# Attention scores: blocks of three and of one share a PSUM bank, value products of those two together, and a new table of leans

## The chip, the cores and the metric

The kernel runs on one core of one Trainium2 chip. The metric is the time in microseconds (us) of one execution on the device. Before the change it is 1697.37 us, the median of three runs (1695.88, 1697.37 and 1698.11).

## What is computed

Four layers act in turn on x, 2048 rows of 512 numbers, each added to its input: attention with a memory, a Fourier mixing, and the two once more. In the reference, cut to what matters:

```
x = x + A(layernorm(x)); x = x + B(layernorm(x))      # twice
A: q, k, v of 32 heads, 16 wide; 4 segments of 512 rows, in turn:
     p     = softmax(q k^T * scale + causal mask)       # inside the segment
     a_mem = phi(q) M / (phi(q) z + 1e-6)
     o     = g * a_mem + (1 - g) * (p v)
     M, z  = M + phi(k)^T v, z + sum phi(k)
   return o wo
B: y = dft_seq_re (x dft_hid_re^T) - dft_seq_im (x dft_hid_im^T)
```

Inside a segment the mask keeps a key block only for the query blocks at and behind it. With blocks of 128 rows there are four key blocks and four query blocks, and a head has ten blocks of scores that count, of the sixteen.

## The kernel before

A segment's 32 heads are worked in four groups of eight; a group is four pairs (p) of two heads (a = 0 or 1). There are 2 layers x 4 segments x 4 groups = 32 groups. Each group's q and k stand in `qst` and `kst` so that head a of a pair lies on partitions from 64a on, and the products of the two heads run side by side in the TensorE's upper and lower rows (called row-tiled below). The scores are computed twice. `s_x` computes them with the queries on the partitions, and the VectorE takes each row's maximum (`t_max`, whose tiles are `junk` and `mx`). One transpose by the TensorE (`identf,mx`) turns the maxima, which then become two more rows of `qst`. `s_st` computes the scores once more with the keys on the partitions, the maximum subtracted. For each PSUM bank the ScalarE takes the exponential into a tile `pt` (in profiles `w`), and the GpSimd sets the masked triangle of each diagonal block to zero (`t_sel`, an affine select).

`s_av` multiplies v by these tiles: 32 output partitions for each pair, four pairs in the four column strips of the array (column-tiled below; `w,vt` in profiles). All four key blocks t of a group add up in one bank `av` for each a. Everything else of the TensorE (projections, the hidden and the sequence DFT, the output projection, each with 128 rows and 128 columns) uses the whole array, in f16 pairs. Matmuls that fill gaps (`onesb`) keep the TensorE's clock up while little work is ready.

A step of `s_x` and of `s_st` fills two banks, one for each a, and both passes walk over t. A product of block t is n = 128 (t+1) columns wide in `s_x`, and n = 512 - 128 t in `s_st`, and a bank of 512 columns takes as many pairs as fit:

```
for t in range(TT):
    n = 512 - 128 * t
    w = 512 // n
    for p0 in range(0, NP, w):
        yield need("T", qs, ks, tag=(kt, kt, "pt", "pt"), mode="h")
```

So the width of 512 takes four steps, 384 takes four, 256 takes two and 128 takes one: 11 steps a group and pass, of which the four of width 384 leave a quarter of their banks empty. `s_av` takes a step for each t and a, that is 8 a group.

The order on every engine is set when the program is built. Streams (`s_...`) and tasks (`t_...`) are Python generators that say which engine, tiles and PSUM banks they need next; a planner with costs and due times (`Plan`) keeps the time at which each is free, and the loop at the end of `body` lets the candidate go that could begin first. The table `LEAN` is subtracted there: a number of planned ns for a stream and an engine's letter (V, A, G, T, Y: VectorE, ScalarE, GpSimd, TensorE, SyncE's DMA queue), positive to be taken earlier, negative later. The planner also charges a change between whole-array, row-tiled and column-tiled work (`mode`). Every instruction is recorded through one helper line (L272 before, L273 after), so rows of the profile are told apart by their tiles.

Of the kernel before, what the change touches and what calls it, by code (L numbers as in the profile page):

```python
# [13 lines left out]
OP = mybir.AluOpType  # L14
# [15 lines left out]
BF16 = mybir.dt.bfloat16  # L30
NEG = -1e30
TICK = 10240 / 3
LEAN = dict(s_stT=150.0, s_memV=40.0, s_wV=80.0, s_rY=150.0, t_mergeA=40.0, s_xA=150.0, t_abA=40.0, t_mergeY=-150.0, s_mV=40.0, t_cV=-40.0, s_cA=-80.0, s_oY=40.0, t_cY=80.0, t_lnG=80.0, t_splitV=-40.0, t_phiA=150.0, s_kV=-300.0, t_mergeV=150.0, s_cT=80.0, s_avT=80.0, s_wA=-150.0, t_resV=-150.0, t_selG=40.0, s_lnY=-150.0, t_rowsY=300.0, t_ktY=-80.0)
APART = dict(pj=(1, 4), av=(1, 2), dft=(0, 2), sx=(2, 4), st=(2, 4), ss=(0, 4))
SHARED = dict(pj=(1, 4), av=(0, 2), dft=(1, 2), sx=(0, 2), st=(0, 2), ss=(2, 6))
HOLD, SWITCH = 700.0, 95.0
# [7 lines left out]
WARM, IDLE, SPARE = 4200, 500.0, 300.0  # L44
DEEP = 1500.0
AHEAD = 2
NR = 2


# [229 lines left out]
def body(ctx: ExitStack, tc: tile.TileContext, x, wq, wk, wv, wo, beta, wd, cs, out):  # L279
# [23 lines left out]
    def ps(kind, dt=F32, shape=(128, 512)):  # L303
        return pl.take(kind, shape, dt)
# [62 lines left out]
    def spawn(g):  # L367
        tasks.append([next(g, None), g, g.__name__])
# [44 lines left out]
    def share(o, src, s):  # L413
# [3 lines left out]
        yield need("VG", o, src)  # L417
        tt(o[:, 1], src, o[:, 0], OP.subtract)

    def flat(t):  # L420
        return t.rearrange("p a b -> p (a b)")

# [228 lines left out]
    def t_merge(e, o, gi, g, n, key):  # L651
        yield gate("GM")
        yield need("V", e, o, gt, tag="md")
        x = sb("md", F32, (128, 2, 512))
        V.transpose(x[:, 0], e)
        yield need("V", x)
        V.transpose(x[:, 1], o)
        pl.close(e, o)
        rc = rg("rc", 4, F32, (128, 2, 16))
        xa = x[:, 0]  # L660

        def view(off, *dims):
            return bass.AP(xa.tensor, xa.offset + off, [list(xa.ap[0])] + [list(d) for d in dims])

        yield need("V", x)
        d = view(16, (496, 2), (32, 16))
        if not gi:
            V.tensor_scalar(rc, d, 1e-6, None, op0=OP.add)
            d = rc
        V.reciprocal(rc, d)  # L670
        yield need("G", rc)
        G.tensor_tensor(rc, rc, gt[:, gi, g, :].unsqueeze(2).to_broadcast([128, 2, 16]), op=OP.mult)
        yield need("VG", rc, x)
        for a in range(2):
            c = slice(16 * a, 16 * a + 16)
            tt(n.rearrange("p (b r) -> p b r", r=32)[:, :, c], view(528 * a, (32, 16), (1, 16)),
               rc[:, a].unsqueeze(2).to_broadcast([128, 16, 16]), OP.mult)
        pl.close(x)
        done.add(key)
# [201 lines left out]
        apart[0] = False  # L881
        kinds.update(SHARED)

    def t_max(sp, mx, a, p0, w, t, left):
        n = 128 * (t + 1)
        for p in range(p0, p0 + w):
            o = (p - p0) * n
            yield need("V", sp)
            junk = rg("junk", 2, BF16)
            V.tensor_tensor_reduce(junk[:, :n], sp[:, o:o + n], cmask[:, 512 - n:], 1.0, -3e38,  # L890
                                   OP.add, OP.max, mx[:, a, p, t:t + 1])
        pl.close(sp)
        left[0] -= 1

    def s_x():
        for i in range(NGRP):
            yield gate(("dq", i), ("dk", i), "CM")
            qs, ks = qst[i % NR], kst[i % NR]
            mx = rg("mx", 2, F32, (128, 2, NP, TT))
            left = [0]  # L900
            kx = scores("x")
            for t in range(TT):
                n = 128 * (t + 1)
                w = 512 // n
                for p0 in range(0, NP, w):
                    yield need("T", qs, ks, tag=(kx, kx), mode="h")
                    sp = [ps(kx), ps(kx)]
                    for p in range(p0, p0 + w):
                        o = (p - p0) * n
                        for a in range(2):  # L910
                            T.matmul(sp[a][:, o:o + n], qs[64 * a:64 * a + 48, p, 128 * t:128 * t + 128],
                                     ks[64 * a:64 * a + 48, p, 0:n], start=True, stop=True)
                    left[0] += 2
                    for a in range(2):
                        spawn(t_max(sp[a], mx, a, p0, w, t, left))
# [12 lines left out]
            for a in range(2):  # L928
                for j in range(2):
                    r = 64 * a + 48 + j  # L930
                    Y.dma_start(qs[r:r + 1].rearrange("o p (t n) -> o (p t) n", t=TT),
                                mhl[16 * a:16 * a + 16, j, :], est=(609, 341, 172))
            done.add(("X", i))

    def t_sel(sp, pt, w, n, f, keys):
        yield need("A", sp)
        A.activation(pt[:, :w * n], sp[:, :w * n], AF.Exp, scale=f)
        pl.close(sp)
        yield need("G", pt)
        v3 = pt[:, :w * n].rearrange("k (w n) -> k w n", w=w)[:, :, 0:128]  # L940
        G.affine_select(v3, v3, pattern=[[0, w], [1, 128]], compare_op=OP.is_ge, fill=0.0,
                        base=0, channel_multiplier=-1)
        for k in keys:
            done.add(k)

    def s_st():
        for i in range(NGRP):
            yield gate(("X", i), "KR")
            qs, ks = qst[i % NR], kst[i % NR]
            kt = scores("t")  # L950
            for t in range(TT):
                n = 512 - 128 * t
                w = 512 // n
                for p0 in range(0, NP, w):
                    yield need("T", qs, ks, tag=(kt, kt, "pt", "pt"), mode="h")
                    sp = [ps(kt), ps(kt)]
                    for p in range(p0, p0 + w):
                        o = (p - p0) * n
                        for a in range(2):
                            T.matmul(sp[a][:, o:o + n], ks[64 * a:64 * a + 50, p, 128 * t:128 * t + 128],  # L960
                                     qs[64 * a:64 * a + 50, p, 128 * t:], start=True, stop=True)
                    for a in range(2):
                        pt = sb("pt")
                        spawn(t_sel(sp[a], pt, w, n, f_s[i % NG], [("pt", i, a, t, p) for p in range(p0, p0 + w)]))
                        for p in range(p0, p0 + w):
                            pts[i, a, t, p] = (pt, pt[:, (p - p0) * n:(p - p0 + 1) * n])
            done.add(("ST", i))

    def s_av():
        for i in range(NGRP):  # L970
            q, g = divmod(i, NG)
            v = vt[i % NR]
            for t in range(TT):
                for a in range(2):
                    yield gate(("v", i), *[("pt", i, a, t, p) for p in range(NP)])
                    tiles = [pts[i, a, t, p] for p in range(NP)]
                    yield need("T", v, *[x[0] for x in tiles], tag="av" if t == 0 else (), mode="v")
                    if t == 0:
                        avs[i, a] = ps("av")
                    av = avs[i, a]  # L980
                    for p in range(NP):
                        T.matmul(av[32 * p:32 * p + 32, 128 * t:],
                                 v[:, t, p].rearrange("k e d -> k (e d)")[:, 16 * a:16 * a + 32], tiles[p][1],
                                 start=(t == 0), stop=(t == TT - 1), skip_group_check=True)
                    for x in {x[0].tensor.name: x[0] for x in tiles}.values():
                        pl.close(x)
            done.add(("E", i))

# [339 lines left out]
```

## Time and profile before

| what | value |
|---|---|
| median of three runs | 1697.37 us |
| profiled execution, its own time | 1699.92 us |
| its span, from first to last instruction | 1698.2 us |
| VectorE, ScalarE, GpSimd busy | 1036.8, 872.3, 810.3 us |
| matmul records of the TensorE | 11145 |
| transposes of maxima on the TensorE: start of the first and the fifth | 48.26 and 185.19 us |

A row of the groups' view names engine, operation, tiles (out<-in), shapes, the count, then busy us and mean ns of one, and the engine's idle time ahead of them. The trace lists each f32 matmul twice (1024 products of v in the program stand as 2048). Matmuls overlap in the pipeline, so the distance between two starts, not the duration shown, is what a matmul takes of the TensorE's time.

### The profile page before, as it was taken

How to read it: one execution, taken by the hardware profiler on the slowest of the kernel's cores; microseconds unless marked ns; L12 is line 12 of the kernel's file. 1: busy time of each engine (PE TensorE's matmuls, PEld its weight loads, DVE VectorE, ACT ScalarE, POOL GpSimd, SP SyncE). 2: the span in 40 equal slices, each digit the busy share in tenths (PEclk: the TensorE clock that was granted, in tenths of full speed). 3: DMA queues.
4: the chain of work that ended last, by engine and by line, in shares of the span. 5: the costliest groups of instructions: out<-in, count | busy, mean ns of one | idle time of the engine just before them, and what ended most of it. 6: DMA issues, size and time to landing. Idle time of an engine off the chain costs nothing.

```text
span 1698.2 us, 32247 instructions
## 1 busy us (share of the span) xinstructions
PE 1662.3 (98%) x11145; PEld 734.7 (43%) x11145; DVE 1036.8 (61%) x3262; ACT 872.3 (51%) x1480; POOL 810.3 (48%) x1445
## 2 busy tenths in 40 slices
PE   8889999999999999999999999999999999999999
PEld 4344344444444344444544444443444444444444
DVE  8784865778677786635768558546575765433221
ACT  5487577755656666535376754655455325312000
POOL 4376556575565556634255644635454415322000
PEclk9789999999999999999999999999999999999999
DMA  7546545655357432525746663543435322131423
GB/s 182 147 116 178 128 132 159 172 142 152 94 148 208 126 119 84 189 56 196 193 148 187 182 179 90 132 116 98 140 91 149 105 85 76 57 125 38 143 70 123
DMA packets 208629, 222.92 MB, mean 131 GB/s; under 512 B 104520, under 2 KB 127048, under 8 KB 208464
## 3 DMA queue, kind: packets, MB, share of 16 engines
q1 hardware_dynamic: 208464, 220.85, 45.8%
q8 instruction: 88, 1.44, 0.4%
q14 instruction: 77, 0.63, 0.1%
HBM read 137.40 MB, written 61.87 MB: 117 GB/s over the span
## 4 chain that ended last, share of the span: by engine, by line
PE 77%; DVE 9%; ACT 5%; issue 4%; DMA 3%; POOL 2%; SPq 1%; ACTq 0%; DVEq 0%; POOLq 0%
PE b L272 77%; ACT w L272 4%; DVE junk L272 4%; SPq L272 1%; DVE w L272 1%; POOL w L272 1%; DMA w<-w 1%; DMA w<-x 1%; DVE m L272 1%; DVE mx L272 1%; DVE y L272 1%; DVE bst L272 0%; DVE cam L272 0%; DMA w<-in_cs_dram 0%; DVE pmax L272 0%
## 5 line engine op out<-in xcount | busy, mean ns | idle before, releaser
L272 PEld LDWEIGHTS <-w 128*128 128x128 f16 x5056 | 467.8, 98 | 612.8 <-issue 101.1
L272 PE MATMUL b<-w,w 128*128 128x512 f16 x3072 | 708.5, 380 | 1.7 <-DVE mx L272 0.8
L272 ACT ACTIVATE w<-b,fac 128x512 f32<-128x512 f32 (+1 forms) x728 | 419.2, 655 | 176.3 <-PE b L272 175.8
L272 DVE CUSTOM_DVE_ANT_0 junk<-b,cmask 128x128 bf16<-128x128 f32 (+3 forms) x1024 | 436.3, 483 | 71.6 <-PE b L272 71.1
L272 POOL TENSOR_TENSOR w<-w,w 128x512 f16<-128x512 f32 (+1 forms) x294 | 347.5, 1187 | 247.1 <-ACT w L272 223.6
L272 POOL TENSOR_SCALAR_AFFINE_SELECT w<-w 128x128 f32<-128x128 f32 (+2 forms) x704 | 237.0, 350 | 202.7 <-ACT w L272 194.1
L272 DVE SCALAR_TENSOR_TENSOR y<-b,fyu,y 128x512 f32<-128x512 f32 x200 | 148.9, 745 | 235.6 <-PE b L272 235.2
L272 ACT ACTIVATE w<-w,csc 128x512 f16<-128x512 f32 (+1 forms) x256 | 180.1, 720 | 41.5 <-DVE csc L272 32.8
L272 PE MATMUL b<-g,w 128*128 128x512 f16 x768 | 183.1, 383 | 3.2 <-DMA g<-w 0.8
L272 PE MATMUL b<-wd,w 128*128 128x512 f16 x768 | 176.8, 379 | 0.1
L272 PE MATMUL b<-w,vt 128*32 128x512 f32 (+3 forms) x2048 | 172.4, 449 | 1.9 <-POOL w L272 1.1
L272 ACT ACTIVATE w<-b 128x512 f16<-128x512 f32 x128 | 75.9, 596 | 189.4 <-PE b L272 179.3
L272 DVE SCALAR_TENSOR_TENSOR w<-b,w 128x512 f16<-128x512 f32 x128 | 87.6, 687 | 120.3 <-ACT w L272 118.7
L272 ACT ACTIVATE w<-w 128x512 f16<-128x512 f32 (+1 forms) x137 | 86.5, 632 | 90.1 <-DVE w L272 87.9
L272 PE MATMUL b<-kst,qst 48*128 48x128 f16 (+3 forms) x1024 | 117.5, 304 | 6.3 <-DVE mx L272 3.2
L272 PE MATMUL b<-qst,kst 50*128 50x512 f16 (+3 forms) x1024 | 115.8, 302 | 5.5 <-DVE mx L272 2.2
L272 PE MATMUL b<-w,g 128*128 128x128 f16 x1536 | 96.3, 221 | 0.0
L272 PEld LDWEIGHTS <-g 128*128 128x128 f16 x1536 | 89.6, 99 | 12.7 <-issue 7.8
L272 DVE STREAM_TRANSPOSE m<-b 128x512 f32<-128x512 f32 x112 | 75.6, 698 | 31.1 <-PE b L272 30.7
L272 PEld LDWEIGHTS b<-w,vt 128*32 128x32 f32 x2048 | 54.8, 110 | 87.7 <-issue 48.2
L272 PE MATMUL b<-wo,w 128*128 128x512 f16 x384 | 89.1, 379 | 0.0
L272 PEld LDWEIGHTS <-kst 50*128 50x128 f16 x1024 | 37.3, 94 | 111.7 <-issue 105.2
(105 smaller groups left out, 1019.3 us busy)
## 6 DMA issues: line engine op xcount, KB each, us to landing
w<-in_cs_dram SPq DMA_DIRECT2D x128, 256.0 KB, 3.5
cc<-w SPq DMA_DIRECT2D x128, 256.0 KB, 3.2
w<-cc SPq DMA_DIRECT2D x128, 256.0 KB, 3.1
w<-w SPq DMA_DIRECT2D x96, 256.0 KB, 3.5
d<-w SPq DMA_DIRECT2D x128, 128.0 KB, 2.5
w<-in_x_dram SPq DMA_DIRECT2D x32, 256.0 KB, 3.6
qst<-d SPq DMA_DIRECT2D x64, 128.0 KB, 2.7
kst<-d SPq DMA_DIRECT2D x64, 128.0 KB, 3.3
```

What stands on the lines that cost most here:

```text
L272: r = f(*args, **kw)
```

## The change

Both passes now have steps of three kinds, built by `steps`: `a` is the block of width 512, one pair a bank; `b` is width 256, two pairs a bank; `c` puts width 384 at column 0 and width 128 of the same pair at column 384. That is 4 + 2 + 4 = 10 steps a group and pass. `s_x` takes them in the order a, b, c, so the widest come first where the narrowest did; `s_st` in the order a, c, b. `s_av` takes a step for each kind and a: 6 a group, and the step of kind c does the products of key blocks 1 and 3 together, 8 matmuls after each other. `t_sel` takes one exponential over the whole bank and one affine select over all the diagonal blocks in it, with a view that steps from column 0 to 384. `view` is only moved out of `t_merge`. In `LEAN`, `t_resV` goes from -150 to -300 and `t_selG` from 40 to -150, `s_lnY` (-150) goes, and `s_mA` (-80), `s_xY` (-40) and `t_yA` (-150) come.

```diff
-LEAN = dict(... t_resV=-150.0, t_selG=40.0, s_lnY=-150.0, t_rowsY=300.0, t_ktY=-80.0)
+LEAN = dict(... t_resV=-300.0, t_selG=-150.0, t_rowsY=300.0, t_ktY=-80.0, s_mA=-80.0, s_xY=-40.0, t_yA=-150.0)
+XORDER, SORDER = "abc", "acb"
...
+    def steps(span):
+        one, two, four = (sorted(range(TT), key=lambda t: span(t)[1])[i] for i in (0, 1, 3))
+        three = 6 - one - two - four
+        return dict(
+            a=[[(four, p, 0)] for p in range(NP)],
+            b=[[(two, p, 0), (two, p + 1, 256)] for p in range(0, NP, 2)],
+            c=[[(three, p, 0), (one, p, 384)] for p in range(NP)])
...
-    def t_sel(sp, pt, w, n, f, keys):
+    def t_sel(sp, pt, items, f, keys):
         yield need("A", sp)
-        A.activation(pt[:, :w * n], sp[:, :w * n], AF.Exp, scale=f)
+        n = items[-1][2] + 512 - 128 * items[-1][0]
+        A.activation(pt[:, :n], sp[:, :n], AF.Exp, scale=f)
         pl.close(sp)
         yield need("G", pt)
-        v3 = pt[:, :w * n].rearrange("k (w n) -> k w n", w=w)[:, :, 0:128]
+        v3 = view(pt, 0, (max(items[-1][2], 1), len(items)), (1, 128))
...
     def s_av():
...
-            for t in range(TT):
+            for k in SORDER:
                 for a in range(2):
-                    yield gate(("v", i), *[("pt", i, a, t, p) for p in range(NP)])
+                    ts = sorted({t for x in SSTEP[k] for t, p, o in x})
+                    yield gate(("v", i), *[("pt", i, a, t, p) for t in ts for p in range(NP)])
```

Counted over the whole order of both programs (a run is a stretch of TensorE matmuls of one tiling):

| | before | after |
|---|---|---|
| steps of each score pass x banks | 352 x 2 | 320 x 2 |
| exponentials of scores on the ScalarE | 704 | 640 |
| affine selects on the GpSimd | 704 | 640 |
| steps of value products | 256 | 192 |
| matmuls that fill gaps (`onesb`, 512 columns) | 83 | 85 |
| row-tiled runs on the TensorE | 378 | 359 |
| column-tiled runs | 119 | 104 |
| whole-array runs | 363 | 354 |

The order of the TensorE, in the middle of the kernel, between the 19th and the 20th transpose of maxima: value products of key block 1 (32x384) of one group, for a = 0 and then a = 1, with `b` the bank `av` and `w` the tiles of exponentials. Before:

```order
L272 MATMUL b_12927<-w_12961,vt_108 32x384
L272 MATMUL b_12927<-w_12967,vt_108 32x384
L272 MATMUL b_12927<-w_13005,vt_108 32x384
L272 MATMUL b_12927<-w_13012,vt_108 32x384
L272 MATMUL b_12935<-w_12962,vt_108 32x384
L272 MATMUL b_12935<-w_12968,vt_108 32x384
L272 MATMUL b_12935<-w_13006,vt_108 32x384
L272 MATMUL b_12935<-w_13013,vt_108 32x384
```

The same place after the change, a = 0 and the first row of a = 1:

```order
L273 MATMUL b_12779<-w_12814,vt_108 32x384
L273 MATMUL b_12779<-w_12830,vt_108 32x384
L273 MATMUL b_12779<-w_12869,vt_108 32x384
L273 MATMUL b_12779<-w_12879,vt_108 32x384
L273 MATMUL b_12779<-w_12814,vt_108 32x128
L273 MATMUL b_12779<-w_12830,vt_108 32x128
L273 MATMUL b_12779<-w_12869,vt_108 32x128
L273 MATMUL b_12779<-w_12879,vt_108 32x128
L273 MATMUL b_12796<-w_12815,vt_108 32x384
```

The four products of key block 3 (32x128), which stood in a later run with those of block 2, now follow those of block 1, and read the same four tiles.

The order of the TensorE near the kernel's start, in the first group's pass for the maxima: a row-tiled step (`kst,qst`; the bank's two heads alternate) and the gap-filling matmuls behind it. Before:

```order
L272 LDWEIGHTS qst_106
L272 MATMUL b_819<-kst_104,qst_106 128x384
L272 LDWEIGHTS qst_106
L272 MATMUL b_820<-kst_104,qst_106 128x384
L272 LDWEIGHTS onesb
L272 MATMUL b_827<-onesb 128x512
L272 LDWEIGHTS onesb
L272 MATMUL b_827<-onesb 128x512
L272 LDWEIGHTS onesb
L272 MATMUL b_827<-onesb 128x512
```

After, a step of kind c there:

```order
L273 LDWEIGHTS qst_106
L273 MATMUL b_811<-kst_104,qst_106 128x384
L273 LDWEIGHTS qst_106
L273 MATMUL b_812<-kst_104,qst_106 128x384
L273 LDWEIGHTS qst_106
L273 MATMUL b_811<-kst_104,qst_106 128x128
L273 LDWEIGHTS qst_106
L273 MATMUL b_812<-kst_104,qst_106 128x128
L273 LDWEIGHTS onesb
L273 MATMUL b_827<-onesb 128x512
```

The products of width 128 (`128x128`), which opened the pass with eight in one step, now stand behind each pair of width 384, in the same two banks.

The order of the GpSimd in the middle of the kernel, one group's selects and the f16 splits (TENSOR_TENSOR) around them. Before, from the last two selects of a group's blocks of width 384 on:

```order
L272 AFFINE_SELECT w_11966<-w_11966 128x128
L272 AFFINE_SELECT w_11967<-w_11967 128x128
L272 TENSOR_TENSOR w_11997<-w_11708,w_11997 128x512
L272 TENSOR_TENSOR w_12013<-w_11733,w_12013 128x512
L272 AFFINE_SELECT w_12022<-w_12022 128x2x128
L272 AFFINE_SELECT w_12023<-w_12023 128x2x128
L272 AFFINE_SELECT w_12037<-w_12037 128x2x128
L272 AFFINE_SELECT w_12038<-w_12038 128x2x128
L272 AFFINE_SELECT w_12055<-w_12055 128x512
L272 AFFINE_SELECT w_12056<-w_12056 128x512
```

After, from the last two selects of the banks of kind c on:

```order
L273 AFFINE_SELECT w_11807<-w_11807 128x2x128
L273 AFFINE_SELECT w_11808<-w_11808 128x2x128
L273 TENSOR_TENSOR w_11842<-w_11253,w_11842 128x512
L273 TENSOR_TENSOR w_11872<-w_11521,w_11872 128x512
L273 AFFINE_SELECT w_11884<-w_11884 128x2x128
L273 AFFINE_SELECT w_11885<-w_11885 128x2x128
L273 AFFINE_SELECT w_11898<-w_11898 128x2x128
L273 AFFINE_SELECT w_11899<-w_11899 128x2x128
L273 TENSOR_TENSOR w_11936<-w_11556,w_11936 128x512
```

The two selects over four blocks (`128x512`) are gone, since the blocks of width 128 now lie beside those of width 384, and those selects cover two blocks each; what stands between them is the same kind of work.

More of the change, by code (lines that the diff above doesn't have):

```diff
@@ L418, in share, with view @@
         tt(o[:, 1], src, o[:, 0], OP.subtract)
+    def view(t, off, *dims):
+        return bass.AP(t.tensor, t.offset + off, [list(t.ap[0])] + [list(d) for d in dims])
     def flat(t):
@@ L659, in t_merge @@
         rc = rg("rc", 4, F32, (128, 2, 16))
-        xa = x[:, 0]
-        def view(off, *dims):
-            return bass.AP(xa.tensor, xa.offset + off, [list(xa.ap[0])] + [list(d) for d in dims])
         yield need("V", x)
-        d = view(16, (496, 2), (32, 16))
+        d = view(x, 16, (496, 2), (32, 16))
         if not gi:
@@ L675, in t_merge @@
             c = slice(16 * a, 16 * a + 16)
-            tt(n.rearrange("p (b r) -> p b r", r=32)[:, :, c], view(528 * a, (32, 16), (1, 16)),
+            tt(n.rearrange("p (b r) -> p b r", r=32)[:, :, c], view(x, 528 * a, (32, 16), (1, 16)),
                rc[:, a].unsqueeze(2).to_broadcast([128, 16, 16]), OP.mult)
@@ L882, in together, with t_max @@
         kinds.update(SHARED)
[L884 to L887, printed above, removed]
+    def steps(span):
[5 more added lines that the diff above has]
+            c=[[(three, p, 0), (one, p, 384)] for p in range(NP)])
+    XSTEP = steps(lambda t: (0, 128 * (t + 1)))
+    SSTEP = steps(lambda t: (128 * t, 512 - 128 * t))
+    def t_max(sp, mx, a, items, left):
+        for t, p, o in items:
+            n = 128 * (t + 1)
             yield need("V", sp)
@@ L901, in s_x @@
             kx = scores("x")
-            for t in range(TT):
[L903 to L913, printed above, removed]
-                    for a in range(2):
-                        spawn(t_max(sp[a], mx, a, p0, w, t, left))
+            for items in [x for k in XORDER for x in XSTEP[k]]:
+                yield need("T", qs, ks, tag=(kx, kx), mode="h")
+                sp = [ps(kx), ps(kx)]
+                for t, p, o in items:
+                    n = 128 * (t + 1)
+                    for a in range(2):
+                        T.matmul(sp[a][:, o:o + n], qs[64 * a:64 * a + 48, p, 128 * t:128 * t + 128],
+                                 ks[64 * a:64 * a + 48, p, 0:n], start=True, stop=True)
+                left[0] += 2
+                for a in range(2):
+                    spawn(t_max(sp[a], mx, a, items, left))
             yield lambda: left[0] == 0
@@ L950, in s_st @@
             kt = scores("t")
[L951 to L961, printed above, removed]
-                    for a in range(2):
[L963 to L966, printed above, removed]
+            for items in [x for k in SORDER for x in SSTEP[k]]:
+                yield need("T", qs, ks, tag=(kt, kt, "pt", "pt"), mode="h")
+                sp = [ps(kt), ps(kt)]
+                for t, p, o in items:
+                    n = 512 - 128 * t
+                    for a in range(2):
+                        T.matmul(sp[a][:, o:o + n], ks[64 * a:64 * a + 50, p, 128 * t:128 * t + 128],
+                                 qs[64 * a:64 * a + 50, p, 128 * t:], start=True, stop=True)
+                for a in range(2):
+                    pt = sb("pt")
+                    spawn(t_sel(sp[a], pt, items, f_s[i % NG], [("pt", i, a, t, p) for t, p, o in items]))
+                    for t, p, o in items:
+                        pts[i, a, t, p] = (pt, pt[:, o:o + 512 - 128 * t])
             done.add(("ST", i))
@@ L972, in s_av @@
             v = vt[i % NR]
-            for t in range(TT):
+            for k in SORDER:
                 for a in range(2):
-                    yield gate(("v", i), *[("pt", i, a, t, p) for p in range(NP)])
-                    tiles = [pts[i, a, t, p] for p in range(NP)]
-                    yield need("T", v, *[x[0] for x in tiles], tag="av" if t == 0 else (), mode="v")
-                    if t == 0:
+                    ts = sorted({t for x in SSTEP[k] for t, p, o in x})
+                    yield gate(("v", i), *[("pt", i, a, t, p) for t in ts for p in range(NP)])
+                    tiles = {(t, p): pts[i, a, t, p] for t in ts for p in range(NP)}
+                    yield need("T", v, *[x[0] for x in tiles.values()], tag="av" if k == SORDER[0] else (), mode="v")
+                    if k == SORDER[0]:
                         avs[i, a] = ps("av")
                     av = avs[i, a]
[L981 to L985, printed above, removed]
+                    for t in ts:
+                        for p in range(NP):
+                            T.matmul(av[32 * p:32 * p + 32, 128 * t:], v[:, t, p].rearrange("k e d -> k (e d)")[:, 16 * a:16 * a + 32], tiles[t, p][1],
+                                     start=(k == SORDER[0]), stop=(k == SORDER[-1] and t == ts[-1]),
+                                     skip_group_check=True)
+                    for x in {x[0].tensor.name: x[0] for x in tiles.values()}.values():
                         pl.close(x)
```

4 lines of the change are left out of this document (2 added, 2 removed).

## The prediction

> **What bounds the kernel now.** First the page: busy time of each engine, and the chain that ended last.
>
> ```profile
> PE 1662.3 (98%) x11145; PEld 734.7 (43%) x11145; DVE 1036.8 (61%) x3262; ACT 872.3 (51%) x1480; POOL 810.3 (48%) x1445
> PE 77%; DVE 9%; ACT 5%; issue 4%; DMA 3%; POOL 2%; SPq 1%; ACTq 0%; DVEq 0%; POOLq 0%
> ```
>
> The matmuls cover 98% of the span and carry 77% of the chain. A share over the whole span hides stages, so next the table by stretch: from the first scores (34 us) to the fifth transpose of maxima (185 us), from there to 1361 us, and the rest.
>
> ```profile
> 34.00:185.00 151.00, 137.43 (x986) 57.65 (x983) 109.97 (x421) 100.74 (x175) 87.68 (x160) 0.89 0.56 149
> 185.00:1361.00 1176.00, 1163.71 (x8152) 514.90 (x8152) 778.66 (x2488) 686.85 (x1165) 643.41 (x1132) 1.00 0.50 140
> 1361.00:1698.20 337.20, 333.22 (x1803) 146.73 (x1803) 117.98 (x266) 64.17 (x111) 62.22 (x124) 1.00 0.28 88
> ```
>
> The columns are us, then busy us and count of PE, PEld, DVE, ACT and POOL, the granted clock, and the DMA. In the long middle PE stands still for 12.3 us of 1176, at full clock. In the start it stands still for 13.6 of 151 us, and the clock is 0.89. The view of waits says for whom PE waited, over the span:
>
> ```profile
> PE b L272 <- DVE mx L272: 10.6, 19, 1.6
> PE b L272 <- ACT w L272: 5.1, 13, 0.9
> PE b L272 <- POOL w L272: 3.0, 9, 0.8
> ```
>
> These are score banks that the VectorE or the ScalarE had not emptied (15.7 us) and value products whose tile GpSimd had not masked (3.0 us). So over the middle the kernel takes as long as PE's queue takes, and what counts is how long the same products occupy PE. The timeline of PE shows it, row after row (start, us, tiles):
>
> ```profile
> 400.32 1.07 PE L272 MATMUL b<-w,vt 128*32 128x256 f32 x16
> 401.33 1.47 PE L272 MATMUL b<-w,w 128*128 128x512 f16 x6
> 402.73 0.55 PE L272 MATMUL b<-kst,qst 48*128 48x384 f16 x4
> 403.21 2.12 PE L272 MATMUL b<-w,w 128*128 128x512 f16 x9
> 405.26 0.64 PE L272 MATMUL b<-w,vt 128*32 128x128 f32 x16
> 405.84 0.60 PE L272 MATMUL b<-kst,qst 48*128 48x512 f16 x4
> 406.37 2.18 PE L272 MATMUL b<-w,g 128*128 128x128 f16 x36
> 408.49 0.39 PE L272 MATMUL b<-kst,qst 48*128 48x512 f16 x2
> 408.81 0.84 PE L272 MATMUL b<-w,g 128*128 128x128 f16 x12
> ```
>
> Six whole-array matmuls last 1.40 us until scores start (401.33 to 402.73), nine last 2.05 us until value products start. Three more cost 0.65, so one is 0.217 us, six are 1.30, and **leaving a whole-array run costs 0.10 us**. Four score products take 0.53 us (405.84 to 406.37), two take 0.32 (408.49 to 408.81): a pair is 0.21, and **leaving a row-tiled run costs 0.11 us**. Value products of 256 columns take 1.01 us, of 128 columns 0.58: half the columns is 0.43 less, so **leaving a column-tiled run costs 0.15 us**. These are differences of few rows with two decimals, good to about 0.02 us.
>
> **The change part by part.** The products themselves stay: the same columns of scores and values, in other companies. What goes is boundaries. By the counts of the order (table above), 378 row-tiled runs become 359, 119 column-tiled 104, and exits from whole-array runs go from 362 to 353. That is 19 x 0.11 = 2.1, 15 x 0.15 = 2.2 and 9 x 0.10 = 0.9 us: **5.2 us less**. The gain is smaller than the 64 score steps and 64 product steps that are saved, since many of these stood side by side already, such as products of 256 and 128 columns in one run. Counted by place, the start up to the fifth transpose has 8 boundaries more (116 to 124), and all behind it 51 fewer (743 to 692). So the saving falls where PE is the queue that sets the time, and a possible extra (0.6 us by the same prices, already in the sum) where PE waits anyway.
>
> The exponentials and selects come next.
>
> ```profile
> L272 ACT ACTIVATE w<-b,fac 128x512 f32<-128x512 f32 x472 | 289.4, 694 | 125.0 <-PE b L272 124.9
> L272 ACT ACTIVATE w<-b,fac 128x384 f32<-128x384 f32 x256 | 130.4, 584 | 51.3 <-PE b L272 50.9
> L272 POOL TENSOR_SCALAR_AFFINE_SELECT w<-w 128x128 f32<-128x128 f32 x512 | 147.0, 299 | 147.0 <-ACT w L272 139.3 <-DMA kst<-d 5.0 <-DMA w<-in_cs_dram 0.5
> L272 POOL TENSOR_SCALAR_AFFINE_SELECT w<-w 128x256 f32<-128x256 f32 x128 | 51.0, 409 | 47.5 <-ACT w L272 47.1
> L272 POOL TENSOR_SCALAR_AFFINE_SELECT w<-w 128x512 f32<-128x512 f32 x64 | 39.4, 638 | 8.2 <-ACT w L272 7.7 <-POOL w L272 0.4
> ACT w L272 <- PE b L272: 355.1, 155, 39.1
> ```
>
> 448 of the 472 wide activations are exponentials (24 belong to phi). A group had 14 x 694 + 8 x 584 ns = 14.4 us and will have 20 x 694 = 13.9: 0.5 us less, 16 over 32 groups. The selects go from 16 x 299 + 4 x 409 + 2 x 638 = 7.7 us to 8 x 299 + 12 x 409 = 7.3. The maxima on the VectorE stay 32 of the same widths. I cost all of it at nothing: the ScalarE waits for PE 355 us anyway. Its upper end is the start, where five groups' exponentials give back 2.5 us if PE waits for nothing else.
>
> One bank in eleven is no longer handed over. Of the 15.7 us that PE waited for emptied banks that would be 1.4 us; it could also turn round, since the merged bank is read twice by the maxima, and I take zero between +1.4 and -1.4. The merged value step waits for eight tiles where a step of four stood. The nearest row is PE's waits for GpSimd: 9 in 256 steps, 0.33 us each. A wait at each of the 64 merged steps would be 21 us, none would give back 3.0. I take zero, by the rate of before; work of other streams, planned around it, covers the tile's way.
>
> The leans move instructions of the other engines past each other: selects, residual adds and some of the ScalarE's copies later, on SyncE's queue the loads of s_ln earlier and the rows of maxima of s_x later. None changes a count. I take zero: queued behind a late select are f16 splits, of which PE hardly waits for any. Without that cover a select behind one split (1159 ns in the row below) is what a product waits for.
>
> ```profile
> L272 POOL TENSOR_TENSOR w<-w,w 128x512 f16<-128x512 f32 x222 | 256.7, 1159 | 191.4 <-ACT w L272 181.4 <-DVE w L272 4.5 <-issue 1.9
> ```
>
> Two more gap-filling matmuls (0.22 us each) stand in gaps: zero. Moving `view` is nothing. Sum: 1699.9 us of the profiled execution less 5.2 is 1694.7. That execution was 2.6 us above the median of the runs, so the median becomes 1697.4 - 5.2 = **1692.2, say 1692 us**.
>
> **The rivals.** A measurement of this kernel tells some 0.2% from no change, 3.4 us: faster is below 1694.0, slower above 1700.8.
>
> *The start loses more clock (slower).* The table of the start, split at the places where the clock changes:
>
> ```profile
> 34.00:54.00 20.00, 18.48 (x113) 7.22 (x111) 19.18 (x94) 4.85 (x8) 4.57 (x4) 1.00 0.86 242
> 54.00:75.00 21.00, 17.23 (x58) 4.84 (x56) 17.71 (x59) 12.01 (x21) 8.33 (x16) 0.59 0.24 80
> 75.00:98.00 23.00, 21.80 (x206) 10.86 (x205) 11.89 (x53) 19.95 (x37) 16.04 (x34) 1.00 0.78 178
> 98.00:130.00 32.00, 28.33 (x202) 11.81 (x201) 26.86 (x110) 25.01 (x43) 23.02 (x45) 0.73 0.29 76
> 130.00:185.00 55.00, 51.58 (x414) 22.91 (x413) 34.33 (x108) 38.92 (x68) 35.72 (x63) 1.00 0.63 173
> ```
>
> Where few matmuls are ready (58 in 21 us), the clock falls to 0.59, then 0.73. In clock time that is 21 x 0.41 + 32 x 0.27 = 17.2 us. The new order of steps thins PE's queue at other places here. If the dips become half as large again, 8.6 us eat the gain and the 3.4 us: slower from there, at about 1702. For it: the gap-filling matmuls placed up to the fourth transpose rise from 54 to 66, so the planner saw more emptiness early. Against it: they are 83 and 85 in all, the VectorE's work for a group is the same, and the ScalarE's is less. The Trainium skill, "TensorE: Matmul & The Clock Gate", Part 1, states that the array is throttled by default and that activity in a window releases it, at half or full clock. By that rule thinner work there would cost time twice, in waiting and in clock; the trace, with 0.59 where PE issued least, agrees.
>
> *The boundaries were free (no change).* A change of tiling takes 0.1 us in which the other engines go on emptying banks; without it PE reaches the next step earlier and waits there. For it: in the middle PE stands still 12.3 us already, and the VectorE is busy 66% of it. Against it: 12.3 us over some 740 boundaries is 0.02 each, so most steps find their bank empty. The gain would shrink to a third or less: 1696. The Trainium skill, "Perfetto Trace Analysis", Identifying the Most-Contended Engine, states that the matmuls' busy share is no measure of how close a kernel is to the TensorE's limit, and that the busy share of weight loads is: 43% here. By that rule PE has room, and the sum would be zero instead of 5.2. The distances between starts in the timeline, 0.217 us a matmul with nothing between, speak against it here.
>
> *The hand-overs count too (much faster).* The start gives 2.5 us (exponentials), the waits 1.4, and the dips shrink by a tenth, 1.7: 1692.2 - 5.6, about 1686.6. For it: PE's waits name emptied banks most. Against: the VectorE, not the ScalarE, is the engine waited for, and its work stays.
>
> That the change doesn't do what it says is excluded by the order, which has the ten steps and the fewer runs.
>
> **How the numbers follow.** Boundaries go and waits stay: 0.45, at 1689 to 1695.5, of which 0.08 lies above 1694. Much faster: 0.20. No change: 0.18. Slower: 0.17. So faster is 0.37 + 0.20 = 0.57, same 0.18 + 0.08 = 0.26, slower 0.17. The range runs from 1683, a few us under the fast rival, to 1703, a little over the slow one's time. It leaves out some 0.08 at each end: the products' waits beyond 11 us, and dips that vanish by half.
>
> **What would show it.** Right: PE's distances as above, and between the fifth transpose and the end of the score groups some 6 us less in PE's own time, while exponentials number 640 at about 694 ns and selects 640. The start's table should keep its clock (0.89 before) within 0.02. Wrong: PE's waits for GpSimd several times 3.0 us (the merged step), a clock under 0.85 in the start (the slow rival), PE's idle time in the middle over 16 us (boundaries were free), or under 8 us (hand-overs).

## The result, and the profile after

The change takes 1687.64 us (median of four runs, 1686.12 to 1690.92), the kernel before, over the same series, 1697.74 us (1695.88 to 1698.18). The ratio is 0.9946, with a 95% interval of 0.9934 to 0.9959: 10.1 us faster by the medians, 9.2 by the ratio (7.0 to 11.2 by its interval), where 5.2 were worked out. The profiled executions lie 13.8 us apart (1699.92 and 1686.12 us): that of before was slower than the four runs of its series, that of after was the fastest of its four. So a difference of the two profiles is more than the change.

The busy times on the page after:

```profile
PE 1651.1 (98%) x11147; PEld 740.2 (44%) x11147; DVE 1041.0 (62%) x3263; ACT 862.1 (51%) x1416; POOL 798.0 (47%) x1380
```

The view of the cores, span and mean granted clock, of before:

```profile
core 0: 1698.2 us, clock 0.989
```

and of after:

```profile
core 0: 1684.3 us, clock 0.994
```

The TensorE stands still for 33.2 us (1684.3 - 1651.1), before for 35.9. The clock is the second difference: 1698.2 x 0.011 = 18.7 us of clock time were lost before, 1684.3 x 0.006 = 10.1 after (with three decimals of the clock, each is good to about 1 us). These two clocks belong to one execution each. By stretch, with the columns and the limits of the table of before:

```profile
34.00:185.00 151.00, 139.18 (x1022) 60.64 (x1019) 110.52 (x397) 104.97 (x174) 92.77 (x160) 0.93 0.58 158
185.00:1361.00 1176.00, 1164.37 (x8220) 522.18 (x8220) 794.50 (x2557) 681.98 (x1122) 630.66 (x1081) 1.00 0.49 140
1361.00:1684.30 323.30, 319.13 (x1708) 141.91 (x1706) 106.03 (x222) 54.60 (x91) 57.37 (x108) 1.00 0.28 89
```

The stretches do not hold the same work in both kernels: the last one is 13.9 us shorter because that work was done earlier. In the start the clock is 0.93 instead of 0.89, and more matmuls run there (1022 for 986). In the middle the TensorE stands still for 11.6 us, before for 12.3. The start once more, at the two dips of the clock:

```profile
54.00:75.00 21.00, 18.06 (x85) 6.02 (x85) 18.51 (x73) 14.08 (x24) 9.00 (x17) 0.67 0.34 107
98.00:130.00 32.00, 26.57 (x206) 11.21 (x195) 26.96 (x126) 27.57 (x46) 26.02 (x44) 0.89 0.36 92
```

They were 0.59 and 0.73. In the first dip 85 matmuls are issued where 58 were. The TensorE's waits, over the span:

```profile
PE b L273 <- DVE mx L273: 8.2, 19, 1.6
PE b L273 <- ACT w L273: 6.2, 20, 0.7
PE b L273 <- POOL w L273: 2.9, 7, 0.8
```

They hardly moved: 14.4 us for emptied banks, 15.7 before, and 2.9 for masked tiles, 3.0 before. The other engines' rows after:

```profile
L273 ACT ACTIVATE w<-b,fac 128x512 f32<-128x512 f32 x664 | 406.5, 693 | 181.5 <-PE b L273 174.6 <-POOL w L273 6.3
L273 POOL TENSOR_SCALAR_AFFINE_SELECT w<-w 128x256 f32<-128x256 f32 x384 | 152.2, 409 | 149.1 <-ACT w L273 144.2 <-issue 2.5 <-PE b L273 0.8
L273 POOL TENSOR_SCALAR_AFFINE_SELECT w<-w 128x128 f32<-128x128 f32 x256 | 72.2, 292 | 84.6 <-ACT w L273 83.0 <-PE b L273 0.7
ACT w L273 <- PE b L273: 373.2, 145, 36.5
```

The exponentials and phi shrank by 13.3 us (16 were worked out), the selects by 13.0 (12.7 worked out), and the ScalarE waits for the TensorE longer than before (373.2 us for 355.1): it was not on the path. The timeline of the TensorE shows the new steps and that a boundary costs what it did:

```profile
908.54 0.39 PE L273 MATMUL b<-kst,qst 48*128 48x256 f16 x4
908.86 1.47 PE L273 MATMUL b<-w,w 128*128 128x512 f16 x6
910.26 0.83 PE L273 MATMUL b<-kst,qst 48*128 48x384 f16 x12
911.03 1.47 PE L273 MATMUL b<-w,w 128*128 128x512 f16 x6
912.43 1.92 PE L273 MATMUL b<-w,vt 128*32 128x512 f32 x16
914.28 0.61 PE L273 MATMUL b<-qst,kst 50*128 50x384 f16 x8
914.83 2.76 PE L273 MATMUL b<-w,w 128*128 128x512 f16 x12
...
1120.23 1.93 PE L273 MATMUL b<-w,vt 128*32 128x384 f32 x32
1122.10 0.61 PE L273 MATMUL b<-qst,kst 50*128 50x256 f16 x8
```

Six whole-array matmuls take 1.40 us to the next start (908.86 to 910.26, 911.03 to 912.43), 0.10 beyond 6 x 0.217, as before. Two steps of kind c (`48x384` and the other widths are merged to one row; `x8` at 914.28) take 0.55 us for 1024 columns side by side, 0.43, so leaving costs 0.12. The merged value products of blocks 1 and 3 take 1.87 us for both heads (1120.23 to 1122.10), 4 x 0.43 and 0.15.

These are single rows. Over the whole of both traces, one can take the time from each run's first start to the next run's and subtract its matmuls, at 0.217 us for 512 columns of f16 and twice that for f32 (runs at full clock; of whole-array runs those that hold only 512-column f16 matmuls; half or a quarter where two heads or four pairs run side by side). The median left over is 0.10 us after whole-array, 0.11 after row-tiled and 0.13 after column-tiled work, in both kernels. With that, 43 boundaries make 4.9 us. The same traces give 859 and 816 changes of tiling, as the order does, when the products with the memory (`w,macc`, 64 rows) are counted as row-tiled too; they do not use the whole array.

So the profiled pair has two parts: 43 boundaries fewer, 5.2 us at the prices of the prediction, and 8.6 us of clock time, 13.8 together against spans 13.9 us apart. That they add up so well is partly chance, since some of the lost clock time falls where the TensorE waits anyway; the experiment without gap fillers, below, weighs that.

And the clock part belongs to this pair more than to the change. The 24 runs of the kernel before in the later series have clocks from 0.989 to 0.996, on average 0.9915; the four of the change have 0.991 to 0.994, on average 0.9925. The profile of before is at the lower end of its scatter, that of after at the upper end. By the averages the lost clock time is 14.5 and 12.7 us, 1.8 apart and not 8.6.

### The profile page after: what moved, and what is told of

The parts are those of the page before. It is cut to its first block, busy times and chain, and to the rows that moved or that the text cites. A ratio compares the mean times of both kernels' runs of the same rounds, so it can differ in the third digit from the quotient of the medians.

```text
span 1684.3 us, 31989 instructions
## 1 busy us (share of the span) xinstructions
PE 1651.1 (98%) x11147; PEld 740.2 (44%) x11147; DVE 1041.0 (62%) x3263; ACT 862.1 (51%) x1416; POOL 798.0 (47%) x1380
## 4 chain that ended last, share of the span: by engine, by line
PE 80%; DVE 7%; ACT 4%; issue 3%; DMA 3%; POOL 3%; SPq 1%; ACTq 0%; POOLq 0%; DVEq 0%
PE b L273 80%; DVE junk L273 3%; ACT w L273 3%; POOL w L273 2%; DMA w<-w 2%; DVE w L273 1%; SPq L273 1%; DVE mx L273 1%; DVE m L273 0%; DVE pmax L273 0%; DVE y L273 0%; DMA w<-cc 0%; POOL rs L273 0%; POOL mv L273 0%; DMA w<-x 0%
## 5 line engine op out<-in xcount | busy, mean ns | idle before, releaser
L273 ACT ACTIVATE w<-b,fac 128x512 f32<-128x512 f32 x664 | 406.5, 693 | 181.5 <-PE b L273 174.6
L273 DVE CUSTOM_DVE_ANT_0 junk<-b,cmask 128x512 bf16<-128x512 f32 (+3 forms) x1024 | 437.3, 484 | 64.0 <-PE b L273 63.1
L273 POOL TENSOR_SCALAR_AFFINE_SELECT w<-w 128x256 f32<-128x256 f32 (+1 forms) x640 | 224.4, 362 | 233.7 <-ACT w L273 227.2
L273 PE MATMUL b<-w,vt 128*32 128x128 f32 (+3 forms) x2048 | 167.7, 445 | 1.1 <-POOL w L273 1.1
L273 PE MATMUL b<-kst,qst 48*128 48x512 f16 (+3 forms) x1024 | 112.5, 302 | 5.3 <-DVE mx L273 2.4
L273 PE MATMUL b<-qst,kst 50*128 50x512 f16 (+3 forms) x1024 | 111.5, 302 | 3.9 <-ACT w L273 1.6
L273 DVE TENSOR_REDUCE cam<-w 128x1 bf16<-128x512 f32 x128 | 81.7, 674 | 10.1 <-DMA w<-in_cs_dram 9.9
```

The lines of the kernel that those rows point to most:

```text
L273: r = f(*args, **kw)
```

## The experiments

Twelve kernels were run: first the parts of the change, one by one, then small changes of the leans and tables that belong to neither kernel, then the clock. Each ratio is to the kernel before in the same series of runs; its medians were 1695.77, 1697.52 and 1697.75 us in the three series. Theory 'boundaries' says that the count of changes of tiling sets the time, theory 'emptiness' that the time in which the TensorE has nothing ready does.

**The change with the old leans** (the table of before in the new kernel):

```diff
-... t_resV=-300.0, t_selG=-150.0, t_rowsY=300.0, t_ktY=-80.0, s_mA=-80.0, s_xY=-40.0, t_yA=-150.0)
+... t_resV=-150.0, t_selG=40.0, s_lnY=-150.0, t_rowsY=300.0, t_ktY=-80.0)
```

> The change with the old table of leans; scores and products as changed. Its TensorE order has 814 changes of tiling (859 before, 816 with the change) and 124 gap-filling matmuls (83 and 85). Theory 'boundaries' (only the count of changes of tiling matters, 0.12 us each): as the change, 1687 to 1689 us. Theory 'emptiness' (what also differs is how long the TensorE has nothing ready near the start, which the gap-filling matmuls mark, 0.22 us each): 39 more of them are 8.5 us, so 1695 to 1698 us. Rival 'clock': the half-clock time of the profile decides, 20 us as with the change or 37 us as before, and the time goes with half of it.

Measured: 1716.09 us, 1.0122 (1.0106 to 1.0137) of before. All three expectations fall by their size; emptiness has the sign against the change. **The old steps with the new leans**, the reverse edit in the kernel before:

> The kernel before with the new table of leans alone. 911 changes of tiling, 82 gap-filling matmuls. 'Boundaries': 52 more than before, 6 us slower than before, about 1704 us. 'Emptiness': also 1704, since the gap fillers are as before. Rival 'the leans made the gain': faster than before, under 1694.

Measured: 1727.59 us, 1.0186 (1.0165 to 1.0206). The rival falls: the new table alone makes the kernel before 32 us slower. Boundaries and emptiness said 6. So each half of the change alone is a loss, of 20 and of 32 us, and the two together a gain of 10.

**The change with a value step for each key block**:

```diff
-            for k in SORDER:
-                for a in range(2):
-                    ts = sorted({t for x in SSTEP[k] for t, p, o in x})
+            parts = [(k, [t]) for k in SORDER for t in sorted({t for x in SSTEP[k] for t, p, o in x})]
+            for n, (k, ts) in enumerate(parts):
+                for a in range(2):
```

> The change, but with a step for each key block in the value products again (8 a group), in the order 0, 1, 3, 2. 807 changes of tiling, 131 gap-filling matmuls. 'Boundaries': 1 us faster than the change, about 1686.5. 'Emptiness': 46 more fillers are 10 us, about 1697. Rival 'the merged products bring the gain': slower than the change by some 2 us (15 column-tiled runs at 0.15).

Measured: 1714.78 us, 1.0117 (1.0102 to 1.0132). **The kernel before with blocks 2 and 3 of the value products together**:

```diff
-            for t in range(TT):
+            for ts in ((0,), (1,), (2, 3)):
```

> The kernel before, old leans and old score steps, with the value products of key blocks 2 and 3 in one step. 845 changes of tiling, 96 gap-filling matmuls. 'Boundaries': 1.7 us faster than before, about 1696. 'Emptiness': 1.7 less and 2.8 more, about 1699. Rival 'the merged products bring the gain': under 1693.

Measured: 1722.18 us, 1.0159 (1.0144 to 1.0175). With the merged products taken from the new kernel and with a pair of them given to the old one, both get slower, by 27 and by 26 us. That is hardly a price of these products: their count of boundaries would make a microsecond or two. What the four kernels so far share is a table of leans that stood with other steps.

**One lean moved by 10 planned ns**, in the changed kernel:

```diff
-LEAN = dict(s_stT=150.0, ...
+LEAN = dict(s_stT=140.0, ...
```

> The change with one lean moved by 10 planned ns (s_stT 150 to 140), which means nothing in itself. TensorE's order is the same until shortly after the fourth transpose of maxima and another from there; 826 changes of tiling, 113 gap fillers. 'Boundaries': 1 us slower than the change, about 1688.5. 'Any other order is slower' (the table fits its one order; what an untried order loses is time in which the TensorE waits, most of it up to 340 us): 1700 to 1716.

Measured: 1710.06 us, 1.0080 (1.0056 to 1.0105). A nudge without meaning costs 22 us. 'Boundaries' (1688.5) falls, 'any other order is slower' holds here. Its stretches of the start and the middle:

```profile
34.00:185.00 151.00, 133.01 (x1006) 58.88 (x1003) 113.64 (x423) 99.56 (x165) 84.33 (x149) 0.91 0.57 158
185.00:1361.00 1176.00, 1158.89 (x8113) 519.22 (x8114) 783.83 (x2486) 680.38 (x1115) 633.01 (x1073) 1.00 0.49 137
```

Its first wait:

```profile
PE b L273 <- DVE mx L273: 17.1, 37, 1.6
```

The TensorE is busy 6 us less in the start and 5 us less in the middle, and waits 17.1 us for maxima, 8.2 in the change.

**The change without the lean t_yA**, whose order differs only from some 230 us on:

```diff
-... s_xY=-40.0, t_yA=-150.0)
+... s_xY=-40.0)
```

> The change without the lean t_yA. TensorE's order is the same until behind the sixth transpose (some 230 us), and another from there; 809 changes of tiling, 85 gap fillers. 'Boundaries': 1 us faster than the change, about 1687. 'Any other order is slower, wherever it differs': 1695 or more. 'The loss sits in the start, where little work is ready': 1685 to 1690, as the start is that of the change.

Measured: 1688.44 us (1686.82 to 1690.32), 0.9951 (0.9935 to 0.9967): as the change. So 'any other order is slower, wherever it differs' falls, and the result speaks for the start. Its five runs have an average clock of 0.9914, no higher than that of before. **The kernel before with another late nudge**, whose order differs from some 620 us on:

```diff
-... s_rY=150.0, ...
+... s_rY=140.0, ...
```

> The kernel before with one lean moved by 10 planned ns (s_rY 150 to 140). TensorE's order is the same until behind the fifteenth transpose (some 620 us); 875 changes of tiling (16 more, 1.9 us), 91 gap fillers (8 more, 1.7 us). 'The loss sits in the start': 1696 to 1702. 'Any other order is slower, wherever it differs': 1705 or more.

Measured: 1708.54 us, 1.0064 (1.0049 to 1.0079). The start theory falls here: neither theory holds for both nudges. The trace says where some of the time went. The stretch holds the second layer's first groups, in the kernel before:

```profile
850.00:1010.00 160.00, 156.34 (x1174) 69.11 (x1173) 107.04 (x373) 107.00 (x184) 93.29 (x174) 0.99 0.61 177
```

and in this one:

```profile
850.00:1010.00 160.00, 154.48 (x1154) 65.62 (x1152) 110.03 (x395) 106.63 (x185) 92.25 (x170) 0.96 0.55 155
```

The clock falls to 0.96 there and the TensorE is busy 1.9 us less. So there may be a second place of the start's kind, where the second layer begins. That is a reading of one profile; no further run tested it.

**Two tables that belong to neither kernel.** Empty (`LEAN = dict()`) in both:

> The kernel before with an empty table of leans. 862 changes of tiling, 108 gap fillers. With bare_after it is the pair in which neither score steps nor products were given a table. 'Any other order is slower': 1710 to 1735, like the other kernels whose table isn't their own. 'Boundaries': as before, 1698.

> The change with an empty table of leans. 796 changes of tiling (66 fewer than bare_before, 7.9 us), 179 gap fillers (71 more, 15.3 us). 'Boundaries': 8 us faster than bare_before. 'Emptiness as the planner sees it': 7 us slower than bare_before. If the steps themselves bring the gain, this is faster than bare_before by 5 to 10 us.

Measured: 1728.51 us with the old steps, 1.0191 (1.0165 to 1.0217), and 1723.77 with the new, 1.0155 (1.0134 to 1.0177). Only the 23 leans that both tables share (`t_resV`, `t_selG`, `s_lnY`, `s_mA`, `s_xY` and `t_yA` left out):

> The kernel before with only the 23 leans that both tables have in common. 883 changes of tiling, 123 gap fillers. 'Any other order is slower': 1705 to 1735. A table that is not fitted to the steps, for the second fair pair.

> The change with the same 23 leans. 815 changes of tiling (68 fewer than common_before, 8.2 us by 0.12 each), 144 gap fillers (21 more, 4.5 us). 'The steps bring 5 us or so, the fitted table the rest': faster than common_before by 2 to 12 us. 'The steps bring nothing, both kernels differ by how well their tables fit': no order between the two, a difference of either sign up to 20 us.

Measured: 1725.51 us with the old steps, 1.0159 (1.0143 to 1.0174), and 1713.92 with the new, 1.0090 (1.0073 to 1.0107). The new steps are faster by 4.7 us with the empty table (the intervals overlap, and 5 to 10 were expected) and by 11.6 with the shared one (they do not overlap, and 2 to 12 were expected). The boundaries would make 7.9 and 8.2. 'Emptiness as the planner sees it', which had the new steps 7 us slower with the empty table, falls.

**The change's order without the gap-filling matmuls**:

```diff
-            T.matmul(p, onesb, onesb.unsqueeze(1).to_broadcast([128, 4, 128]), start=True, stop=True)
+            pl.op("T", "matmul", (p, onesb, onesb.unsqueeze(1).to_broadcast([128, 4, 128])), {})
```

The planner books them, the TensorE doesn't get them.

> The change with its order kept, but without the 85 gap-filling matmuls (no output depends on them). The time with the fillers has 20.5 us at half clock in the profile. 'Clock': more of the start at half clock, 30 to 60 us in all, and the time goes up by a quarter to a half of what is added, so 1690 to 1705. 'The start waits for the other engines, the clock hides behind it': within 3 us of the change, however the clock falls.

Measured: 1692.84 us (1690.41 to 1695.8), 0.9970 (0.9959 to 0.9981) of before, so 5.2 us slower than the change by the medians and 4.1 by the ratios, whose intervals meet at 0.9959.

Its span and clock, its busy times, and then its start:

```profile
core 0: 1691.1 us, clock 0.987
```

```profile
PE 1638.0 (97%) x11062; PEld 734.5 (43%) x11062; DVE 1042.1 (62%) x3263; ACT 862.5 (51%) x1416; POOL 800.2 (47%) x1380
```

```profile
34.00:185.00 151.00, 129.05 (x948) 55.83 (x946) 107.12 (x381) 101.22 (x168) 88.85 (x155) 0.86 0.56 151
```

The lost clock time is 1691.1 x 0.013 = 22.0 us, 11.9 more than with the fillers, and 4.1 to 6.8 us of it (ratios and spans) reach the end. Here all runs agree: the seven clocks are 0.983 to 0.987, those of the change 0.991 to 0.994. The fillers left their gaps behind: the TensorE's idle time is 53.1 us (1691.1 - 1638.0), and with the fillers it was 33.2 of idle time and 18.4 of fillers (85 x 0.216). What grew are the other matmuls, from 1632.7 to 1638.0 us. 'Clock' holds with its 1690 to 1705; 'it hides behind the other engines', within 3 us, is unlikely but not excluded. Between a third and a little over a half of the lost clock time counts. The 24 runs of the kernel before agree: in them a microsecond of lost clock time goes with some 0.4 us of time.

## Why the prediction was right, and where its sizes were off

*The bound.* Right: in the middle the TensorE is busy all but 11.6 of 1176 us, and the kernel got faster by more than its boundaries while the ScalarE's waits for the TensorE grew.

*The boundaries, 5.2 us.* Right, as far as a single pair of traces can show it: the counts are those of the order, the prices are the same in both traces and make 4.9 us (the 0.15 after column-tiled work was a little high), and the idle time of the middle did not take the place of what went (11.6 for 12.3 us), which the rival 'the boundaries were free' required. The 43% of weight loads on which that rival leaned are no room: from 1500 to 1600 us of the kernel before, the TensorE takes 465 matmuls in 100 us and is never idle, and weight loads are busy 45% there. The two pairs with a common table agree in sign. The sign that was named, some 6 us less between the fifth transpose and the end of the score groups, can't be read off, since the fifth transpose starts at 199.10 us now (185.19 before) with more other work ahead of it; but behind it lie 692 changes of tiling, and 743 before. That it is the new steps, not the table, that lower the count shows in the orders: 796 to 826 boundaries in all kernels with new steps, 845 to 911 in those with old ones, whatever their table.

*Exponentials, selects, the merged wait: zero.* Right. The ScalarE's waits for the TensorE grew, and the merged value step waited no more often for GpSimd (7 times 2.9 us in all, 9 times 3.0 before).

*The start, no change.* In the profiled pair it did change: the prediction had the clock of the start stay within 0.02 of 0.89, and expected the change, if any, downwards, since gap fillers and boundaries rose up to the fifth transpose. It rose to 0.93, and the idle time there fell from 13.6 to 11.8 us. But the pair is at both ends of the scatter, and the 1.8 us by which the averages of the lost clock time differ are worth some 0.9 at a half. So runs without a profile do not show that the change made the start's clock better, and the unprofiled start may well be as forecast.

*What the sum lacks.* Boundaries and clock give 5.2 + 0.9 = 6.1 us of the 10.1 (9.2 by the ratio, 7.0 at least). **The sum was too small, and which zero of it is the wrong one stays open**: 1 to 5 us come from elsewhere. In the pair the TensorE's idle time fell by 2.7 us, of which waits for emptied banks are 1.3 (15.7 - 14.4), close to the 1.4 that the prediction weighed and put at zero; how much of that other runs have, no run shows. The fast rival, 'the hand-overs count too', named these waits, but its split can't be tested on one pair.

*The leans, zero.* **The step's reason was wrong, and only the sum of a fitted pair hid it; that the total came out is luck in this term.** It argued that a lean changes no count and that other work covers what is moved. Yet with the old steps the new table alone takes the changes of tiling from 859 to 911, and with the new steps it takes the gap fillers from 124 to 85. Measured ratios to the kernel before show what leans are worth:

| table | old steps | new steps |
|---|---|---|
| that of before | 1 | 1.0122 |
| that of the change | 1.0186 | 0.9946 |
| none | 1.0191 | 1.0155 |
| the shared 23 | 1.0159 | 1.0090 |

The steps with their own table are 24 to 35 us faster than with any of the others, and with any of the others they are 15 to 32 us slower than the kernel before, be it the other kernel's table or an empty one. The new leans are no gain of 28 us on top of the steps; they restore the fit that the new steps take away. That each table was fitted to its steps is read from these ratios; no run shows how a table was made.

The profiles show which part of the time the steps move and which the table. Count as empty the TensorE's idle time and its gap fillers (0.216 us each, an estimate that holds at full clock), and as work the rest of its busy time. The busy times of the six other kernels, in the order of the table below (the kernels before and after are shown above):

```profile
PE 1667.2 (97%) x11186; PEld 746.6 (44%) x11186; DVE 1046.5 (61%) x3267; ACT 859.7 (50%) x1416; POOL 794.6 (46%) x1376
PE 1682.5 (97%) x11144; PEld 734.1 (42%) x11144; DVE 1041.7 (60%) x3263; ACT 877.0 (51%) x1480; POOL 811.6 (47%) x1444
PE 1671.1 (97%) x11170; PEld 734.2 (43%) x11170; DVE 1049.9 (61%) x3270; ACT 874.8 (51%) x1481; POOL 802.9 (47%) x1436
PE 1675.7 (97%) x11241; PEld 752.0 (44%) x11241; DVE 1050.9 (61%) x3268; ACT 862.5 (50%) x1416; POOL 796.6 (46%) x1375
PE 1678.9 (97%) x11185; PEld 738.3 (43%) x11185; DVE 1041.0 (60%) x3268; ACT 872.6 (51%) x1480; POOL 805.8 (47%) x1439
PE 1671.0 (98%) x11206; PEld 747.0 (44%) x11206; DVE 1050.9 (61%) x3276; ACT 862.2 (50%) x1416; POOL 792.1 (46%) x1367
```

| table | steps | span | empty | work |
|---|---|---|---|---|
| that of before | old | 1698.2 | 53.8 | 1644.4 |
| | new | 1715.5 | 75.1 | 1640.4 |
| that of the change | old | 1730.3 | 65.5 | 1664.8 |
| | new | 1684.3 | 51.6 | 1632.7 |
| none | old | 1721.4 | 73.6 | 1647.8 |
| | new | 1722.4 | 85.4 | 1637.0 |
| the shared 23 | old | 1723.5 | 71.2 | 1652.3 |
| | new | 1713.8 | 73.9 | 1639.9 |

With every table the new steps have less work time, and it is under 1641 us in all eight kernels that have them and above 1644 in all six that do not. Only with its own table is a kernel's empty time near 52 to 54 us; with any other of these it is 65 to 85. The change without `t_yA`, as fast as the change, has 55.5 us of it, the slower late nudge 60.0. So the steps take work off the TensorE's queue, and the table decides how much of the queue stays empty. The work time falls by more than the boundaries' prices in three of the four pairs (10.8 us for 7.9 with no table, 12.4 for 8.2 with the shared one); slower clock and short waits are in it too, and no run parts them.

What is lost without it can be summed up for the early nudge against the change, whose spans are 23.2 us apart: 28 more gap fillers at 0.216 us make 6.0, the clock 1707.5 x 0.009 - 10.1 = 5.3, 10 boundaries 1.2. The busy times on its page, and its span and clock:

```profile
PE 1661.1 (97%) x11175; PEld 745.4 (44%) x11175; DVE 1047.1 (61%) x3267; ACT 864.4 (51%) x1416; POOL 799.1 (47%) x1376
```

```profile
core 0: 1707.5 us, clock 0.991
```

The TensorE's idle time grows from 33.2 to 46.4 us (1707.5 - 1661.1), so by 13.2. Together that is 25.7, a little too much, as clock time and idle time overlap. By the count above, empty time is 70.8 us here (51.6 in the change) and work 1636.7. No single wait carries it. Why a change of 10 planned ns turns into that is open: the plan's times and the chip's part somewhere, but no run looked for the place.

*Why the estimate of the risk was off.* The slow rival put its price on the start, which is one place where an unfitted order loses (6 us of busy TensorE in the early nudge), but not the only one, as the late nudge shows. It saw the danger in fewer ready matmuls, and read it off the number of gap fillers. That number alone told little: 85 fillers stand in kernels of 1687 and 1688 us, 82 and 83 in kernels of 1728 and 1698. Idle time has to be added, which only a profile gives.

## What to carry to other kernels

Where one engine's queue is full, count the instructions' boundaries by kind in the order of both programs and price them from distances between starts; here that gave 5 of the 9 to 10 us. Where two profiles differ in the clock, look at the clocks of all runs first: here a single pair showed 8.6 us of lost clock time where the averages differ by 1.8. Where a planner with fitted leans sets the order, judge a change of the work with a refitted table, or with tables fitted to neither version: here the change alone is 20 us slower and the refitted one 10 us faster. A nudge of one lean by an amount that means nothing shows how large that effect is.

## What the runs showed of the hardware

In these two kernels a change of tiling costs the TensorE 0.10 us after whole-array work, 0.11 after row-tiled and 0.13 after column-tiled work (medians over the traces). Weight loads that are busy 45% go with a TensorE that is never idle, where 465 matmuls start in 100 us. And matmuls that compute nothing pay for themselves: with 85 of them in its gaps the changed kernel is 4.1 to 5.2 us faster than without, and its average clock is 0.9925 instead of 0.9857. Between executions of one and the same kernel the clock goes from 0.989 to 0.996.
